# A linear-attention and feed-forward kernel: the last tile's stores issued from ScalarE, the first k and v in 64 partitions, and the casts of k^T v and of w_out's units in other places

## The chip, the core and the metric

The kernel runs on one core of a Trainium2 chip. A core has a matrix engine (TensorE, called PE in the profile; its weight loads are listed apart as PEld), VectorE (DVE), ScalarE (ACT), GpSimd (POOL) and SyncE (SP), which here does nothing but issue transfers. Each engine runs its own instructions in the order of the program, and waits on semaphores for the others. The metric is the device time of one execution in microseconds (us).

## The reference

```python
kv = np.einsum('bhsd,bhse->bhde', k, v)              # b=8, h=8, s=576, d=64
out = np.einsum('bhsd,bhde->bhse', q, kv)
rms = np.sqrt(np.mean(out * out, axis=-1, keepdims=True) + 1e-06)
attn = out / rms * g_norm
x = attn.transpose(0, 2, 1, 3).reshape(4608, 512)
h = x @ w_in                                          # 512 x 2048
sp = np.where(h > 20.0, h, np.log1p(np.exp(np.minimum(h, 20.0))))
g = h * np.tanh(sp)                                   # mish
return (g @ w_out).astype(np.float32)                 # 2048 x 512
```

Linear attention over 8 batches of 8 heads, a norm over each head's 64 channels, and a feed-forward of 4608 tokens with mish between its two products. w_in and w_out are float64, which the kernel reads as pairs of 32-bit words; all else is float32.

## The kernel before

**Tiles.** The 4608 tokens go in 9 tiles of 512 (NT = 9). In the first part of the program each tile goes through x @ w_in and mish, and the result g is stored to DRAM (the tiles gd). The second part, from about 530 us on, loads g again and multiplies it by w_out. A product of two 32-bit matrices is made of three matmuls with each operand split into a high part (ACT, CAST, L117) and a low rest (DVE, subtraction, L118). On top of this each product is a Strassen-Winograd scheme: 7 products of half-size blocks instead of 8, with sums of blocks made before and after.

**Slots.** A tile has 4 groups of 7 products, so NS = 28 slots. The schedule is written by hand: slot(t) first runs what `then(t, ...)` has put down (copies and additions that empty a PSUM bank), then its product (12 matmuls for each of two columns, L471 in `mm_in`), then what `at(t, ...)` has put down. That order is the order of every engine's queue. In a group, `p0` to `p6` leave copies behind: ACT copies the bank a to ula (L434, block 11), the bank bc to ur (L439, block 22) and a to ur (L448, block 12); DVE adds a later bank on top of each (L491), ACT takes the mish (L114). `put_in` then stores the blocks to gd: ula (L494), ur (L497) and ulb (L489). The products that accumulate further in bank a wait for the copy at L448.

**Attention.** That of tile j is computed within tile j-1's slots: loads of q (L280), transposes (L285), q times kv (L308 to L313), squares (L318), the sums over a head by PE (L335 to L346), and at slot 16 the reciprocal root by ACT's Ln and Exp (L357, L358), which need another function table than mish: a table load stands before Ln (L356) and another before the next mish (L114). k^T v of batch b is made two tiles ahead: `kv_load` (L211, L212) loads k and v of two heads in 128 partitions and a rest in 64, `kv_product` (L232) multiplies, `kv_keep` brings the result from PSUM to kv in two halves of partitions, each with a cast (L117, ACT) and a rest (L118, DVE); for the first batches it copies to kvf (L249).

**w_out.** It is prepared in 16 units, spread over tiles 1 to 7, at the slots in `places`. A unit has seven steps: load (L134), scale (L139, ACT), join (L144 to L146, DVE: two words become a float), differences (L154 to L156, DVE), blocks and sums (casts wst<-wx and wst<-w on ACT, rests on DVE), and store (wod<-wst, L198, SP). The pools wx and wst have one buffer, so a unit's first cast waits until the store of the unit before has landed. w_in's units j = 0 to 7 go through the same steps at the start, into buffers wf, which stay in use to the end of tile 8. There are eight wf buffers; after the last use of a pair `wo_load` loads w_out's finished forms into them (wf<-wod, L662). The first block of 256 tokens of the second part (s = 0) is multiplied at L790 within the last tile, the others at L708.

**Queues.** All transfers before are issued by SP, in program order. Each takes one of eight semaphores in turn, and waits for the transfer eight before it to land.

Of the kernel before, what the change touches and what calls it, by code (L numbers as in the profile page):

```python
# [7 lines left out]
F32 = mybir.dt.float32  # L8
# [18 lines left out]
def linear_attention_rms_mish_ffn(  # L27
# [33 lines left out]
    nc = tc.nc  # L61
# [62 lines left out]
    def weight_forms(srcs, m, n, room, forms, put=None):  # L124

        st = {}
        w = m * n

        def load():
            t = room()  # L130
            n_ = 4 // len(srcs)
            for i, src in enumerate(srcs):
                dst = t[:, i].rearrange("p (m n) t -> p m (n t)", m=m) if n_ == 1 else t[:, n_ * i:n_ * i + n_].rearrange("p b n t -> p b (n t)")
                nc.sync.dma_start(dst, src)  # L134
            st["w"] = t.rearrange("p b n t -> p (b n) t")
# [12 lines left out]
        def differences():  # L148
            x = st["x"].rearrange("p (b n) -> p b n", b=4)
            if put:  # L150
                d = st["w"].rearrange("p n t -> p (n t)").bitcast(F32)[:, 0:4 * w].rearrange("p (b n) -> p b n", b=4)
            else:
                d = pools["wd"].tile([P, 4, w], F32, name="wd")
            nc.vector.tensor_sub(d[:, 0:2], x[:, 1:4:2], x[:, 0:2])  # L154
            nc.vector.tensor_sub(d[:, 2], x[:, 3], d[:, 0])
            nc.vector.tensor_sub(d[:, 3], x[:, 2], d[:, 2])  # L156
            st["x"], st["d"] = x, d
# [7 lines left out]
        def blocks():  # L165
            parts(B11, B11 + 1, st["x"][:, 0:1])
            parts(B21, B22 + 1, st["x"][:, 2:4])
# [316 lines left out]
    def put_in(st, block, bank, t):  # L484
        o, i, n = u_dst(st, block), st["i"], st["n"]
        left, right = gd[i][:, 2 * n:2 * n + 2, :], gd[i][:, NF2 + 2 * n:NF2 + 2 * n + 2, :]
        if block == "21":
            mish(o, bank)
            at(t + 2, lambda: nc.sync.dma_start(left[:, :, TH:T], o))  # L489
            return  # L490
        nc.vector.tensor_add(o, bank, o)  # L491
        if block == "11":
            then(t + 1, lambda: mish(o, o))
            at(t + 3, lambda: nc.sync.dma_start(left[:, :, 0:TH], o))  # L494
        elif block == "22":
            then(t + 1, lambda: mish(st["r"], st["r"]))
            at(t + 3, lambda: nc.sync.dma_start(right, st["r"]))  # L497
# [9 lines left out]
    rooms = [up.tile([P, 4, CM * D], F32, name="ur") for _ in range(2)]  # L507
    rooms += [x[:, 2 * u:2 * u + 2].rearrange("p a (h n) -> p (a h) n", h=2) for u in range(2)]
    rrooms = [up.tile([SL, 4, D], F32, name=n) for n in ("ula", "ula", "ulb", "ulb")]

    early = {j: wfp.tile([P, 4, 2 * P, 2], U32, name="wf") for j in range(1, 4)}
    early_q = wfp.tile([P, 2, T // R * D], F32, name="wf")
# [4 lines left out]
    conv = {j: weight_in(j, (lambda j=j: early[j]) if 0 < j < 4 else w64_room) for j in range(NF2)}  # L517
# [41 lines left out]
    kv_product(0, 0, 4, *kv0[0])  # L559
# [320 lines left out]
```

## Time and profile before

| what | us |
|---|---|
| median of 3 runs | 900.79 |
| lowest, highest | 899.94, 905.96 |
| the profiled execution, whole | 899.57 |
| its span on the core | 897.8 |
| PE busy in it | 831.1 |
| DVE busy | 613.7 |
| ACT busy | 459.2 |

A row of a timeline has the start, the time, the engine, the line, the operation and the tiles written and read, with how many instructions went into the row; in brackets stands the idle time of that engine before it, and what ended it. A row of the waits has the engine and line that waited, what released it, and three numbers: us in total, times, and the longest. A granted clock (PEclk) under 1.00 means that PE ran part of that stretch at a lower clock. The chain of work that ended last runs in PE's second part almost without a break.

### The profile page before, as it was taken

What the parts mean: (1) busy time and instruction counts of PE and PEld (TensorE: products, weight loads), DVE (VectorE), ACT (ScalarE), POOL (GpSimd) and SP (SyncE); (2) the same over time, 40 slices, a digit from 0 to 9 for tenths busy, and PEclk for the clock granted to TensorE, in tenths of its full rate; (3) what the DMA queues carried; (4) which work ended last, traced back from release to release, by engine and by line L of the source; (5) the groups of instructions that cost most, each with busy time, mean ns of one, the idle gap of its engine ahead of it and who ended that gap; (6) DMA issues with size and microseconds to landing.
All of it is one profiled execution on the core that took longest, in us unless ns stands there. A gap on an engine that the chain in (4) does not pass through costs nothing. (4 is left out here: it accounts for less than half of the span.)

```text
span 897.8 us, 17035 instructions
## 1 busy us (share of the span) xinstructions
PE 831.1 (93%) x6940; PEld 796.0 (89%) x6940; DVE 613.7 (68%) x808; ACT 459.2 (51%) x698; POOL 4.3 (0%) x21
## 2 busy tenths in 40 slices
PE   1678899998999999999999699999999999999997
PEld 1366699888999999999899699999999999999997
DVE  4688675776767767676765258877676767777672
ACT  2465656566576655666675244443444443443441
POOL 1000000000000000000000000000000000000000
PEclk9988999998999999999999899999999999999999
DMA  9958598978879796867657996333444344333421
GB/s 242 264 149 234 171 279 248 263 231 248 268 235 293 230 268 194 234 206 202 205 173 239 408 376 226 119 118 118 151 153 144 118 135 124 118 118 120 157 77 48
DMA packets 157134, 177.41 MB, mean 198 GB/s; under 512 B 18752, under 2 KB 138560, under 8 KB 156032
## 3 DMA queue, kind: packets, MB, share of 16 engines
q1 hardware_dynamic: 157056, 176.33, 64.8%
q8 instruction: 54, 0.88, 0.4%
q14 instruction: 24, 0.20, 0.1%
HBM read 114.30 MB, written 62.00 MB: 196 GB/s over the span
## 5 line engine op out<-in xcount | busy, mean ns | idle before, releaser
L708 PE MATMUL a<-wf,gf 128*128 128x256 f32 x1632 | 201.8, 283 | 0.5 <-DVE ur L739 0.5
L708 PEld LDWEIGHTS a<-wf,gf 128*128 128x128 f32 x1632 | 198.4, 192 | 0.7 <-DVE ur L739 0.7
L118 DVE TENSOR_TENSOR gf<-g,gf 128x1024 fp32r<-128x1024 f32 (+1 forms) x123 | 132.8, 1087 | 88.0 <-ACT gf L117 88.0
L471 PE MATMUL a<-gf,wf 128*128 128x256 f32 x1296 | 177.3, 291 | 12.2 <-ACT ur L448 9.4
L471 PEld LDWEIGHTS a<-gf,wf 128*128 128x128 f32 x1296 | 166.5, 197 | 20.0 <-ACT ur L448 11.5
L471 PE MATMUL bc<-gf,wf 128*128 128x256 f32 x1296 | 170.8, 286 | 8.4 <-ACT ur L439 7.4
L471 PEld LDWEIGHTS bc<-gf,wf 128*128 128x128 f32 x1296 | 162.4, 192 | 10.1 <-ACT ur L439 7.6
L117 ACT CAST gf<-g 128x1024 fp32r<-128x1024 f32 (+1 forms) x123 | 114.4, 939 | 90.6 <-DVE g L688 65.1
L708 PE MATMUL bc<-wf,gf 128*128 128x256 f32 x1224 | 152.7, 283 | 0.1
L708 PEld LDWEIGHTS bc<-wf,gf 128*128 128x128 f32 x1224 | 149.4, 192 | 0.3 <-ACT gf L117 0.3
L471 PE MATMUL a<-a,wf 128*128 128x256 f32 x432 | 59.3, 288 | 6.2 <-DVE ur L491 6.2
L471 PEld LDWEIGHTS a<-a,wf 128*128 128x128 f32 x432 | 55.9, 194 | 10.0 <-DVE ur L491 4.9
L114 ACT ACTIVATE ur<-ur 128x1024 f32<-128x1024 f32 x36 | 38.1, 1059 | 40.4 <-DVE ur L491 40.2
L118 DVE TENSOR_TENSOR fa<-fl,fh 128x1024 fp32r<-128x1024 f32 x28 | 34.2, 1222 | 22.1 <-ACT fh L117 21.2
L118 DVE TENSOR_TENSOR gf<-gf 128x512 fp32r<-128x512 f32 x45 | 30.4, 689 | 23.9 <-ACT gf L117 23.9
L439 ACT COPY ur<-bc 128x512 f32<-128x512 f32 (+1 forms) x53 | 27.4, 517 | 36.1 <-PE bc L708 22.7
L117 ACT CAST gf<-a 128x1024 fp32r<-128x1024 f32 x17 | 17.9, 1052 | 53.3 <-DVE a L685 53.3
L448 ACT COPY ur<-a 128x512 f32<-128x512 f32 (+1 forms) x53 | 27.4, 517 | 32.9 <-PE a L708 24.6
L117 ACT CAST gf<-gf 128x512 fp32r<-128x512 f32 x45 | 27.1, 619 | 32.3 <-DVE gf L395 19.1
L491 DVE TENSOR_TENSOR ula<-bc,ula 128x512 f32<-128x512 f32 x36 | 24.7, 687 | 23.5 <-PE bc L471 18.2
L114 ACT ACTIVATE ula<-ula 128x512 f32<-128x512 f32 x36 | 22.8, 632 | 29.7 <-DVE ula L491 29.6
L117 ACT CAST fh<-fl 128x1024 fp32r<-128x1024 f32 x28 | 29.4, 1048 | 0.0
(134 smaller groups left out, 842.0 us busy)
## 6 DMA issues: line engine op xcount, KB each, us to landing
g<-gd SPq DMA_DIRECT2D x18, 2048.0 KB, 8.7
gd<-ur SPq DMA_DIRECT2D x36, 512.0 KB, 4.5
wod<-wst SPq DMA_DIRECT2D x16, 896.0 KB, 6.9
wf<-wod SPq DMA_DIRECT2D x8, 1792.0 KB, 15.0
gd<-ula SPq DMA_DIRECT2D x36, 256.0 KB, 4.6
gd<-ulb SPq DMA_DIRECT2D x36, 256.0 KB, 5.0
w<-in_moe_w_out_dram SPq DMA_DIRECT2D x32, 256.0 KB, 5.2
km<-in_k_dram SPq DMA_DIRECT2D x28, 256.0 KB, 4.6
```

What stands on the lines that cost most here:

```text
L114: nc.scalar.activation(o, i, AF.Mish)
L117: nc.scalar.copy(hi, src)
L118: nc.vector.tensor_sub(lo, src, hi.bitcast(F32))
L439: then(t + 2, lambda: nc.scalar.copy(dst(st, "22"), st["c"]))
L448: then(t + 4, lambda: nc.scalar.copy(dst(st, "12"), st["a"]))
L471: nc.tensor.matmul(bank[:, jj], w[:, right, a, kc, :], xf[:, b, kc, :], start=first and jj == kc == s == 0, stop=(kc == 1 and s == 2), ski ...
L491: nc.vector.tensor_add(o, bank, o)
L708: nc.tensor.matmul(bank, gf[:, a, c, :], wo[c][:, right, b, :], start=first and c == s == 0, stop=(c == NF2 - 1 and s == 2), skip_group_ch ...
```

## The change

There are four parts.

1. The first batch's k and v (b = 0) are loaded by `kv_first` for four heads at a time: 64 partitions, each with 9 tokens in a row (2304 bytes), one transfer each for k and v, into wf buffers that are free at that time. `kv_first_product` multiplies 9 chunks of 64 rows. Before, four heads came as 4 chunks of 128 rows in 1024-byte rows and a rest of 64 rows in 256-byte rows, into buffers of ur, ula, gf and ulb. w_in's units are loaded in 2 transfers of 512 KB instead of 4 of 256 KB, and the sums and blocks of a unit read the blocks in the new order. In ACT's order the sums of w_in's unit 1 and the first square stand ahead of the second copy of kv.
2. `kv_keep` makes both casts first and then both rests; from batch 3 on the loads, the products and the keep stand earlier (the keep at slot 11 instead of 14).
3. w_out's units have their blocks, sums and store a slot earlier; units at slot 15 have join, differences, blocks, sums and store at +1, +2, +4, +4 and +7.
4. The last tile's twelve stores to gd are issued by ACT.

```diff
 def weight_forms(srcs, m, n, room, forms, put=None):
...
-            n_ = 4 // len(srcs)
-            for i, src in enumerate(srcs):
-                dst = t[:, i].rearrange("p (m n) t -> p m (n t)", m=m) if n_ == 1 else t[:, n_ * i:n_ * i + n_].rearrange("p b n t -> p b (n t)")
-                nc.sync.dma_start(dst, src)
+            for src, places in srcs:
+                nc.sync.dma_start(t[:, places].rearrange("p b (m n) t -> p (b m) (n t)", m=m), src)
...
+    def kv_first(h0):
+        ts = []
+        for src in (k, v):
+            t = wfp.tile([S // 9, 4, 9 * D], F32, name="wf")
+            nc.sync.dma_start(t, src[0, h0:h0 + 4].rearrange("h (p c) d -> p h (c d)", c=9))
+            ts.append(t)
+        return ts
+
+    def kv_first_product(h0, kt, vt):
+        for i in range(2):
+            for c in range(9):
+                for o in range(2):
+                    d = slice(c * D, (c + 1) * D)
+                    nc.tensor.matmul(kvps[o * D:(o + 1) * D, 0, h0 // 2 + i, :], kt[:, 2 * i + o, d], vt[:, 2 * i + o, d], start=(c == 0), stop=(c == 8))
...
+        t = kvt[b % 2]
         for r in (slice(0, D), slice(D, P)):
-            if b >= T32 - 1:
-                split(kvt[b % 2][r, 0, n, r], kvt[b % 2][r, 1, n, r], kvps[r, b % 2, n, :])
+            nc.scalar.copy(t[r, 0, n, r], kvps[r, b % 2, n, :])
+        for r in (slice(0, D), slice(D, P)):
+            nc.vector.tensor_sub(t[r, 1, n, r], kvps[r, b % 2, n, :], t[r, 0, n, r].bitcast(F32))
...
+        eng = nc.sync if i < NT - 1 else nc.scalar
...
-            at(t + 3, lambda: nc.sync.dma_start(left[:, :, 0:TH], o))
+            at(t + 3, lambda: eng.dma_start(left[:, :, 0:TH], o))
...
-    weights(1, DIFF, BLOCKS)
-    kv_product(0, 4, 4, *kv0[1])
+    weights(1, DIFF, BLOCKS, SUMS)
+    do(0, 0, "square")
+    kv_first_product(4, *kv0[1])
     kv_keep(0, slice(2, 4))
-    do(0, 0, "square", "sums")
-    weights(1, SUMS)
+    do(0, 0, "sums")
...
-        loads = (5, 6, 14, 16) if b == 2 else (20 - NS, 22 - NS, 5, 8) if b == 3 else (11 - NS, 15 - NS, 5, 8)
+        loads = (5, 6, 14, 16) if b == 2 else (20 - NS, 22 - NS, 4, 6) if b == 3 else (8 - NS, 10 - NS, 4, 6)
...
-            at(t + ((12, 14, 16, 18) if b == 2 else (3, 6, 9, 12))[p], lambda b=b, p=p: k_product(b, p))
-        at(t + (20 if b == 2 else 14), lambda b=b: kv_keep(b, slice(0, NKC)))
+            at(t + ((12, 14, 16, 18) if b == 2 else (2, 4, 6, 8))[p], lambda b=b, p=p: k_product(b, p))
+        at(t + (20 if b == 2 else 11), lambda b=b: kv_keep(b, slice(0, NKC)))
...
-        for s, n in zip(range(7), (-12, 0, 0, 1, 2, 3, 5)):
+    places = [(NS * j + n, (0, 1, 2, 4, 4, 7) if n == 15 else (0, 0, 1, 1, 2, 4)) for j in range(1, NT - 1) for n in ((6, 13, 20) if j < 3 else (9, 15))]
+    for i, (t, ns) in enumerate(places):
+        for s, n in zip(range(7), (-12,) + ns):
```

In the order of the instructions the change shows at three places. The first is ACT at the start: kvf is k^T v of the first batch (s is its PSUM tile), wf takes the forms of w_in's units 0 and 1, fa the square of the first tile's attention. Before:

```order
L249 COPY kvf_181<-s_122 64x2x64 x2
L117 CAST wf<-fl 128x256
L117 CAST wf<-fl 128x2x256
L117 CAST wf<-wd 128x4x256
L139 ACTIVATE fl<-wf 128x1024
L117 CAST wf<-fl 128x256
L117 CAST wf<-fl 128x2x256
L249 COPY kvf_181<-s_122 64x2x64 x2
L318 ACTIVATE fa<-x_247 128x1024
L117 CAST wf<-wd 128x4x256
```

After the change:

```order
L263 COPY kvf_167<-s_122 64x2x64 x2
L117 CAST wf<-fl 128x256
L117 CAST wf<-fl 128x2x256
L117 CAST wf<-wd 128x4x256
L138 ACTIVATE fl<-wf 128x1024
L117 CAST wf<-fl 128x256
L117 CAST wf<-fl 128x2x256
L117 CAST wf<-wd 128x4x256
L336 ACTIVATE fa<-x_249 128x1024
L263 COPY kvf_167<-s_122 64x2x64 x2
```

The second copy of kvf went behind the last cast of unit 1 and the square.

The second place is ACT in tile 1, around Ln and Exp. kv is k^T v of a later batch, wx and w hold a w_out unit, wst its forms; ur, ula and ulb are the blocks of g. Before:

```order
L117 CAST kv_187<-s_122 64x4x64 x2
L114 ACTIVATE ur<-ur 128x1024
L434 COPY ula<-a 128x512
L117 CAST wst<-wx 128x128
L117 CAST wst<-wx 128x2x128
L439 COPY ur<-bc 128x2x256
L356 ACT_TABLE_LOAD
L357 ACTIVATE fl<-ss,eps 8x512
L358 ACTIVATE fl<-fl 8x512
L117 CAST wst<-w_1157 128x4x128
L114 ACT_TABLE_LOAD
L114 ACTIVATE ulb<-a 128x512
```

After the change:

```order
L138 ACTIVATE wx<-w_1167 128x512
L117 CAST wst<-wx 128x128
L117 CAST wst<-wx 128x2x128
L114 ACTIVATE ur<-ur 128x1024
L452 COPY ula<-a 128x512
L117 CAST wst<-w_1167 128x4x128
L457 COPY ur<-bc 128x2x256
L374 ACT_TABLE_LOAD
L375 ACTIVATE fl<-ss,eps 8x512
L376 ACTIVATE fl<-fl 8x512
L114 ACT_TABLE_LOAD
L114 ACTIVATE ulb<-a 128x512
```

The kv casts went ahead of the piece, to where the group before ends; the casts wst<-wx went from behind the copy of ula to ahead of the mish, and the cast wst<-w from between Exp and the table load to ahead of the copy ur<-bc.

The third place is SP at the start of the last tile, whose g is gd_102. Before:

```order
L667 DMA g<-gd_94 128x16x256 x2
L494 DMA gd_102<-ula 128x2x256
L662 DMA wf<-wod_103 128x3584
L662 DMA wf<-wod_104 128x3584
L497 DMA gd_102<-ur 128x1024
L489 DMA gd_102<-ulb 128x2x256
L494 DMA gd_102<-ula 128x2x256
L662 DMA wf<-wod_105 128x3584
L662 DMA wf<-wod_106 128x3584
L497 DMA gd_102<-ur 128x1024
```

After the change:

```order
L679 DMA g<-gd_94 128x16x256 x2
L674 DMA wf<-wod_103 128x3584
L674 DMA wf<-wod_104 128x3584
L674 DMA wf<-wod_105 128x3584
L674 DMA wf<-wod_106 128x3584
L674 DMA wf<-wod_107 128x3584
L674 DMA wf<-wod_108 128x3584
L674 DMA wf<-wod_109 128x3584
L674 DMA wf<-wod_110 128x3584
```

and the stores stand in ACT's queue among the copies that fill and empty the same buffers (PSUM banks a and bc):

```order
L452 COPY ula<-a 128x512
L513 DMA gd_102<-ula 128x2x256
L457 COPY ur<-bc 128x2x256
L114 ACTIVATE ulb<-a 128x512
L516 DMA gd_102<-ur 128x1024
L466 COPY ur<-a 128x2x256
L508 DMA gd_102<-ulb 128x2x256
```

Twelve stores left SP, where they had stood between the loads of g and of wf, for ACT.

More of the change, by code (lines that the diff above doesn't have):

```diff
@@ L153, in differences @@
                 d = pools["wd"].tile([P, 4, w], F32, name="wd")
-            nc.vector.tensor_sub(d[:, 0:2], x[:, 1:4:2], x[:, 0:2])
+            nc.vector.tensor_sub(d[:, 0:2], x[:, 2:4], x[:, 0:4:2])
             nc.vector.tensor_sub(d[:, 2], x[:, 3], d[:, 0])
-            nc.vector.tensor_sub(d[:, 3], x[:, 2], d[:, 2])
+            nc.vector.tensor_sub(d[:, 3], x[:, 1], d[:, 2])
             st["x"], st["d"] = x, d
@@ L166, in blocks @@
             parts(B11, B11 + 1, st["x"][:, 0:1])
-            parts(B21, B22 + 1, st["x"][:, 2:4])
+            parts(B21, B22 + 1, st["x"][:, 1:4:2])
         def sums():
@@ L183, in weight_in @@
         srcs = []
-        for kh, r in ((0, 0), (0, 1), (1, 0), (1, 1)):
+        for r in range(2):
             c0 = 2 * P * (j + r * NF2)
-            src = w_in[kh * 2 * P:(kh + 1) * 2 * P, c0:c0 + 2 * P]
-            srcs.append(src.rearrange("(m p) n -> p m n", p=P))
+            srcs.append((w_in[:, c0:c0 + 2 * P].rearrange("(m p) n -> p m n", p=P), slice(2 * r, 2 * r + 2)))
         return weight_forms(srcs, 2, P, room, forms)
@@ L201, in weight_out @@
             f0 = (c + fh * NF2) * P
-            srcs.append(w_out[f0:f0 + P, :].rearrange("p (r h n) -> p r h n", r=2, h=2)[:, :, h, :])
+            srcs.append((w_out[f0:f0 + P, :].rearrange("p (r h n) -> p r h n", r=2, h=2)[:, :, h, :], slice(fh, 4, 2)))
         return weight_forms(srcs, 1, P, room, forms, store)
@@ L249, in kv_keep @@
                 nc.scalar.copy(kvf[b][r, n, r], kvps[r, b % 2, n, :])
+        if b < T32 - 1:
+            return
+        t = kvt[b % 2]
         for r in (slice(0, D), slice(D, P)):
-            if b >= T32 - 1:
-                split(kvt[b % 2][r, 0, n, r], kvt[b % 2][r, 1, n, r], kvps[r, b % 2, n, :])
+            nc.scalar.copy(t[r, 0, n, r], kvps[r, b % 2, n, :])
+        for r in (slice(0, D), slice(D, P)):
+            nc.vector.tensor_sub(t[r, 1, n, r], kvps[r, b % 2, n, :], t[r, 0, n, r].bitcast(F32))
     def segments(j):
@@ L488, in put_in @@
             mish(o, bank)
-            at(t + 2, lambda: nc.sync.dma_start(left[:, :, TH:T], o))
+            at(t + 2, lambda: eng.dma_start(left[:, :, TH:T], o))
             return
@@ L506, in linear_attention_rms_mish_ffn, with wf_room @@
     open_pools(wst, ("w64", 1), ("wd", 1), ("kvf", 1))
[L507 to L512, printed above, removed]
     def w64_room():
         return pools["w64"].tile([P, 4, 2 * P, 2], U32, name="w64")
-    conv = {j: weight_in(j, (lambda j=j: early[j]) if 0 < j < 4 else w64_room) for j in range(NF2)}
+    def wf_room():
+        return wfp.tile([P, 4, 2 * P, 2], U32, name="wf")
+    conv = {j: weight_in(j, wf_room if 0 < j < 4 else w64_room) for j in range(NF2)}
     LOAD, SCALE, JOIN, DIFF, BLOCKS, SUMS, STORE = range(7)
@@ L532, in linear_attention_rms_mish_ffn @@
     nc.scalar.preload_act_table_set("natural_log_exp_and_others")
-    kv0 = []
-    def k_first(n):
-        kv0.append(kv_load(nc.sync, 0, 4 * n, 4, [t for m in range(2) for t in (rooms[2 * n + m], rrooms[2 * n + m])]))
     weights(0, LOAD)
-    k_first(0)
+    kv0 = [kv_first(0)]
     weights(1, LOAD)
     do(0, 0, "load")
-    k_first(1)
-    units[0][1]["load"](early_q)
+    kv0.append(kv_first(4))
+    units[0][1]["load"](wfp.tile([P, 2, T // R * D], F32, name="wf"))
     for r in (slice(0, D), slice(D, P)):
@@ L558, in linear_attention_rms_mish_ffn @@
     weights(0, SCALE, JOIN)
-    kv_product(0, 0, 4, *kv0[0])
+    kv_first_product(0, *kv0[0])
     kv_keep(0, slice(0, 2))
@@ L635, in linear_attention_rms_mish_ffn @@
     at(NS - 2, out_pools)
-    places = [NS * j + n for j in range(1, NT - 1) for n in ((6, 13, 20) if j < 3 else (9, 15))]
-    for i, t in enumerate(places):
-        for s, n in zip(range(7), (-12, 0, 0, 1, 2, 3, 5)):
+    places = [(NS * j + n, (0, 1, 2, 4, 4, 7) if n == 15 else (0, 0, 1, 1, 2, 4)) for j in range(1, NT - 1) for n in ((6, 13, 20) if j < 3 else (9, 15))]
+    for i, (t, ns) in enumerate(places):
+        for s, n in zip(range(7), (-12,) + ns):
             def run(i=i, s=s):
```

2 lines of the change are left out of this document (1 added, 1 removed).

## Prediction

> **What bounds the kernel now.** I read the busy times first, then a table of stretches of the span, then what TensorE (PE) waits for, then the timeline around each long wait.
>
> ```profile
> span 897.8 us, 17035 instructions
> PE 831.1 (93%) x6940; PEld 796.0 (89%) x6940; DVE 613.7 (68%) x808; ACT 459.2 (51%) x698; POOL 4.3 (0%) x21
> ```
>
> The change takes no matmul of the big products away, so all that can be won is PE's 67 us of idle time and its half-speed stretches. Where they lie, by stretch (start:end, length, busy us of each engine with its instruction count, granted PE clock, DMA share, GB/s):
>
> ```profile
> core 0: us, PE busy (x) PEld busy (x) DVE busy (x) ACT busy (x) POOL busy (x), PEclk, DMA share, GB/s
> 0.00:50.00 50.00, 19.31 (x160) 11.70 (x160) 30.02 (x41) 21.84 (x33) 4.32 (x21) 1.00 0.99 249
> 50.00:118.00 68.00, 57.97 (x447) 47.84 (x448) 55.10 (x74) 38.52 (x58) 0.00 (x0) 0.87 0.67 189
> 118.00:186.00 68.00, 65.15 (x580) 61.96 (x578) 48.41 (x76) 42.20 (x69) 0.00 (x0) 0.97 0.90 269
> 186.00:254.00 68.00, 64.00 (x562) 60.65 (x559) 47.19 (x77) 41.13 (x67) 0.00 (x0) 0.95 0.84 246
> 254.00:322.00 68.00, 67.17 (x601) 63.88 (x600) 48.06 (x75) 43.92 (x70) 0.00 (x0) 1.00 0.81 242
> ...
> 390.00:458.00 68.00, 65.79 (x512) 62.25 (x512) 49.66 (x74) 44.10 (x70) 0.00 (x0) 1.00 0.61 184
> 458.00:526.00 68.00, 58.57 (x468) 57.75 (x467) 28.42 (x49) 32.04 (x55) 0.00 (x0) 0.95 0.85 303
> ...
> 600.00:898.00 298.00, 292.47 (x2436) 292.07 (x2434) 202.48 (x200) 118.34 (x155) 0.00 (x0) 1.00 0.39 119
> ```
>
> The reader should see five different places: a start that is bound by DMA (share 0.99), a stretch short of work and clock up to 118, two stretches (tiles 1 and 2) with about 3 and 4 us idle and a lower clock, tiles 3 to 7 nearly full, and 9.4 us idle in the last tile. The long tail is full and the change leaves it alone. What PE waited for (us in total, times, longest):
>
> ```profile
> PE s L232 <- DMA ur<-in_v_dram: 11.9, 1, 11.9
> PE a L471 <- ACT ur L448: 9.4, 8, 3.6
> ...
> PE bc L471 <- ACT ur L439: 7.4, 1, 7.4
> ...
> PE s L232 <- DMA vm<-in_v_dram: 4.9, 1, 4.9
> ```
>
> Each of the four parts of the change aims at one of these lines.
>
> **Part 1: first k and v in 64 partitions.** It moves the same 1.18 MB for each of the two groups of four heads, as 2 transfers into 64 partitions instead of 4 into 128 and 64. Transfers into few partitions show in the trace: 15 to 18 us is the load of q into 32 partitions, 30 to 33 that of w_in into 128, 7 to 12 holds k and v as they are now.
>
> ```profile
> 7.00:12.00 5.00, 0.07 (x2) 0.10 (x4) 3.08 (x3) 1.12 (x1) 0.00 (x0) 1.00 1.10 291
> 15.00:18.00 3.00, 0.00 (x0) 0.00 (x0) 1.63 (x3) 2.94 (x6) 0.00 (x0) 1.00 1.03 228
> 30.00:33.00 3.00, 1.95 (x4) 0.68 (x4) 2.10 (x2) 2.45 (x4) 0.00 (x0) 1.00 1.00 320
> ```
>
> 1.18 MB takes 4.1 us at 291 GB/s, 5.2 at 228 and 3.7 at 320: from -0.4 to +1.1 a group. I take +1.1, because q's rows have long packets and few partitions, as the new loads have. [...]
>
> The product of four heads goes from 40 records (4 chunks of 128 rows and a rest, for each pair) to 72 of 64 rows:
>
> ```profile
> 11.93 1.12 PE L232 MATMUL s<-ur 128*64 128x64 f32 x16 [11.93 <-DMA ur<-in_v_dram]
> 12.98 0.48 PE L232 MATMUL s<-ula 64*64 64x64 f32 x4
> ```
>
> At 1.12/16 = 0.07 us each 72 cost 5.0 us, without the change of shape, which is the excess of the second row (0.48 for 4, against 0.28), 4.2; before it was 1.12+0.48 twice, about 3.0. So +1.2 to +2.0 for the first group. The first unit's sums and the squares stand ahead of the second copy of kv afterwards, and no longer wait for its product; that covers the second product's longer run and most of the first's delay. What is left is the load time: two groups late by 1.1 each push the wait on vm (4.9 us) by 2.2, and about half of that is absorbed, because the chain behind it up to 71 us is held by VectorE (DVE), not by PE. I take **+1.0**, with ends -0.8 (both groups at 320 GB/s) and +4.6 (1.1 of load and 1.2 of product for each group, nothing absorbed).
>
> **Part 2 in the stretch 50 to 118, and w_in in half as many transfers.** ScalarE (ACT) no longer waits between the two halves of the kv cast. The other waits there are loads and DVE, which stay, so of the 3.2 us of that wait (row 149.66 below) only a quarter is counted: **-0.8** (-2 to +1).
>
> **Parts 2 and 3 in tiles 1 and 2.** ACT's timeline in tile 1, up to the copy PE waits for (start, us, in brackets the idle time before and its releaser), the matmuls around that copy, those around it in tile 2, a long and a short wait in the last tile, the issue of tile 1's store of w_out's forms and the landing of all such stores:
>
> ```profile
> 149.66 0.37 ACT L117 CAST kv<-s 64x256 fp32r<-64x256 f32 x1 [3.23 <-DVE kv L118]
> ...
> 151.14 0.59 ACT L434 COPY ula<-a 128x512 f32<-128x512 f32 x1
> 152.56 0.61 ACT L117 CAST wst<-wx 128x128 fp32r<-128x128 f32 x2 [0.84 <-DMA wod<-wst]
> ...
> 156.22 0.60 ACT L117 CAST wst<-w 128x512 fp32r<-128x512 f32 x1
> ...
> 158.62 0.58 ACT L448 COPY ur<-a 128x512 f32<-128x512 f32 x1
> ```
> ```profile
> 159.26 4.62 PE L471 MATMUL a<-gf,wf 128*128 128x256 f32 x24 [2.48 <-ACT ur L448]
> ...
> 208.46 3.04 PE L471 MATMUL bc<-gf,wf 128*128 128x256 f32 x24
> 215.06 5.49 PE L471 MATMUL a<-gf,wf 128*128 128x256 f32 x24 [3.56 <-ACT ur L448]
> ...
> 510.48 2.93 PE L471 MATMUL bc<-gf,wf 128*128 128x256 f32 x12 [7.44 <-ACT ur L439]
> ...
> 517.64 1.69 PE L471 MATMUL bc<-gf,wf 128*128 128x256 f32 x12 [0.95 <-DVE ula L491]
> ```
> ```profile
> 147.10 0.60 SPq L198 DMA_DIRECT2D wod<-wst  x1
> ```
> ```profile
> DMA to landing us min/median/max: 4.9/6.9/8.9
> ```
>
> The whole stake: 2.48 + 3.56 = 6.0 us idle, and 24 matmuls at 4.62 and 5.49 instead of 3.04, 1.6 + 2.4 = 4.0 more; together 10.0. The clock falls behind the long waits and not behind the wait of 0.95.
>
> The kv casts go to a place where ACT is idle, which frees 3.2 us. But the casts wst<-wx now stand ahead of the mish, of the copy ula<-a and of the copy ur<-bc, and they still wait for the store of the unit before, since wst has one buffer. Casts and store are each a slot earlier. The store took 5.5 us (issued 147.1, by the bracket of row 152.56 landed by 152.56); issued near 146 it lands at 150.9 at the least. From there: two casts 0.61, mish 1.06, copy 0.59, cast wst<-w 0.60, copy ur<-bc 0.58, then tables, Ln and Exp without the cast, 3.9, and ulb 0.5: the copy ur<-a starts near 158.4 instead of 158.62. So one wait takes the place of the other. In tile 2 the same sum gives 0.6. Idle: -0.9 in all. But PE now loses the time in two pieces, at ur<-bc and at ur<-a, of about 1 and 1.5 us, and shorter waits did not lower the clock; I count two thirds of the 4.0: -2.6. Together **-3.5**, ends -10.0 (the store lands before the casts want it) and +1.5 (it lands at 8.9 behind the moved loads of k and v).
>
> **Parts 2 and 3 in tiles 3 to 7.** From 254 to 458 PE waited thus:
>
> ```profile
> PE a L471 <- ACT ur L448: 2.4, 5, 0.6
> ```
>
> By the stretches above the idle time there is 0.8 in one and 2.2 in another. These waits stand behind the kv casts (3.2) and the cast beside Exp (0.6), which both go; the later offsets at slot 15 leave ACT free there. **-2.5** (-3.5 to +1).
>
> **Part 4: the last tile.** A store on SP stood behind two loads of g, 2 MB each, and two loads wf<-wod; ACT waited for its landing, and PE for ACT:
>
> ```profile
> 486.77 5.84 SPq L494 DMA_DIRECT2D gd<-ula  x1
> ...
> 493.93 0.44 SPq L497 DMA_DIRECT2D gd<-ur  x1
> ```
> ```profile
> 509.84 0.58 ACT L439 COPY ur<-bc 128x512 f32<-128x512 f32 x1 [9.98 <-DMA gd<-ur]
> ```
> ```profile
> 484.00:545.00 61.00, 51.71 (x411) 50.90 (x410) 24.86 (x57) 24.29 (x50) 0.00 (x0) 0.94 1.01 379
> 503.00:510.50 7.50, 0.06 (x2) 0.02 (x1) 0.00 (x0) 0.66 (x2) 0.00 (x0) 0.79 1.04 415
> ```
> ```profile
> g<-gd SPq DMA_DIRECT2D x18, 2048.0 KB, 8.7
> ...
> wf<-wod SPq DMA_DIRECT2D x8, 1792.0 KB, 15.0
> ```
>
> Issued from ACT the stores pass SP's backlog. At stake are 7.44 us and the half clock behind it, 2.93 instead of 1.6, 8.8 together. But DMA is full for those 61 us, and the last products of the first block need the last wf<-wod. 61 us at 379 GB/s are 23.1 MB; at 415, the best stretch, 55.7 us: the last load can come at most 5.3 us earlier, and at 395 2.5. PE wins its 8.8 before and gives most back ahead of the last products. [...] ACT takes over 12 issues of about 0.4 us in return; they lie in its idle time (51% busy). I take **-2.5**, ends -5.3 and, with ACT held by its own stores as SP was for 5.84, +3.
>
> **Sum.** +1.0 - 0.8 - 3.5 - 2.5 - 2.5 = -8.3. The profiled execution took 899.57 (span 897.8 and 1.8 around it), 1.2 under the median of the runs, 900.79: 891.3, so **891 us**.
>
> **Rivals.** (a) *The stalls go whole.* The store lands before the casts want it, and the loads move at 415 GB/s: -10.0 and -5.3 instead of -3.5 and -2.5, 899.57 + 1.0 - 0.8 - 10.0 - 2.5 - 5.3 = 882. For it: ACT has 3.2 us more in each tile. Against it: the bracket of row 152.56, and the DMA share.
>
> (b) *The change doesn't do what it says.* The wait for the store keeps tiles 1 and 2 as they were, clock included, and the last tile gives all back: 899.57 + 1.0 - 0.8 - 2.5 = 897. For it: the replay, which won only 0.2 and 0.6 of idle time.
>
> (c) *Slower: ACT is held by its own stores.* In the program's order each transfer has one of eight semaphores, in turn, and waits at the head of its engine's queue for the transfer eight before it; SP stood 5.84 us in this way at a store. Where ACT's stores share a semaphore with wf<-wod (15.0 us to land), ACT stands, with the copies behind it. Of a hold of 9.98 PE lost 7.44, so a hold of 15.0 costs 12.5, and 1.3 of clock. Two of them: 27.6 against 8.8 before, +19, with -5.8 from the other terms 913. It decides for slower by over 1% from two holds of 13.6 us on (24.8 of loss, +16).
>
> (d) *The 64-partition loads cost their upper end*, +4.6 and the stretch behind it +1, with (b) elsewhere: 899.57 + 4.6 + 1.0 - 2.5 = 903. Against it: ACT's new order, which takes the second product off the path.
>
> **Chances.** Forecast 0.47 (its own terms, 886 to 896); (a) 0.20; (b) 0.21; (c) 0.06; (d) 0.06. The range reaches into (a) and over (b): 882.5 to 899. One per cent, 9 us, is about what a measurement of this kernel can tell from no change: faster is below 891.8, half of the forecast's case and all of (a), 0.45; slower is (c) and a bit of (d), 0.08; the same 0.47.
>
> **What would show it.** Start: the first k^T v later than 11.93 by 1.1; sooner, and the loads were fast. Tiles 1 and 2: two waits of 1 to 1.5 us each in place of 2.48 and 3.56, the 24 matmuls behind at about 3.0; a wait of the casts wst<-wx on wod. Last tile: no wait of 7.4 us near 503, one of some us ahead of the last products of the first block, on wf<-wod. The prediction is wrong if ACT stands at an issue in the last tile, or if the casts find their buffer free.

## The result and the profile after

The changed kernel takes 893.22 us (median of 7 runs, 892.54 to 894.53), and 0.990 of the time before (95% interval 0.988 to 0.992). The ratio is taken from undisturbed runs alone, so it does not follow from the median of all seven runs of before beside it, 904.73. The prediction was 891. The profiled execution took 892.98 (span 891.2), 6.6 us less than that of before, where the prediction's sum said 8.3.

The page of the changed kernel, its busy times:

```profile
span 891.2 us, 17127 instructions
PE 829.7 (93%) x7004; PEld 796.6 (89%) x7004; DVE 614.2 (69%) x808; ACT 460.8 (52%) x698; POOL 4.3 (0%) x21
```

PE's busy time is nearly the same (831.1 before, with 64 small matmuls fewer); its idle time fell from 67 to 61.5 us. What PE waited for in the changed kernel (us in total, times, longest):

```profile
PE s L228 <- DMA wf<-in_v_dram: 13.2, 1, 13.2
...
PE s L246 <- DMA vm<-in_v_dram: 6.6, 3, 5.5
PE a L489 <- ACT ur L466: 4.7, 4, 2.0
...
PE bc L489 <- ACT ur L457: 2.4, 1, 2.4
PE a L489 <- ACT ula L452: 2.2, 2, 1.4
...
PE bc L720 <- DVE gf L118: 1.3, 2, 0.8
```

Read beside the list of before: the copy of a (now L466) went from 9.4 to 4.7, the copy of bc (L457) from 7.4 to 2.4. The first load went up from 11.9 to 13.2 and that of vm from 4.9 to 6.6. Two lines are new: the copy to ula, and the low rests that DVE makes (L118) in the second part.

How much that is, stage by stage, shows best by counting. The first part has 3024 matmuls of x and w_in in both traces, the second 2856 at its main line, so the n-th of one can be set against the n-th of the other. The table has the start of a matmul (us) and how long each stretch took, changed minus before:

| up to | before | changed | stretch | predicted |
|---|---|---|---|---|
| first matmul of x and w_in | 40.64 | 41.66 | +1.02 | +1.0 |
| tile 1 | 120.91 | 120.96 | -0.97 | -0.8 |
| tile 3 | 232.00 | 229.36 | -2.69 | -3.5 |
| tile 8 | 476.55 | 472.49 | -1.41 | -2.5 |
| first matmul of s = 1 | 549.00 | 540.76 | -4.18 | -2.5 |
| its 169th | 569.51 | 562.69 | +1.42 | |
| the last | 892.71 | 885.90 | +0.01 | 0 |

### The profile page after: what moved, and what is told of

Read it like the earlier page. It is cut to its first block, busy times and chain, and to the rows that moved or that the text cites. A ratio compares the mean times of both kernels' runs of the same rounds, so it can differ in the third digit from the quotient of the medians.

```text
span 891.2 us, 17127 instructions
## 1 busy us (share of the span) xinstructions
PE 829.7 (93%) x7004; PEld 796.6 (89%) x7004; DVE 614.2 (69%) x808; ACT 460.8 (52%) x698; POOL 4.3 (0%) x21
## 4 chain that ended last, share of the span: by engine, by line
PE 65%; DMA 10%; DVE 10%; ACT 8%; issue 4%; SPq 1%; ACTq 0%; DVEq 0%
PE a L720 21%; PE bc L720 16%; PE a L489 14%; PE bc L489 8%; DMA gd<-ula 4%; PE s L246 2%; DVE ur L510 1%; DMA wf<-in_v_dram 1%; DMA gd<-ur 1%; DMA w<-in_moe_w_in_dram 1%; DMA vm<-in_v_dram 1%; DVE gf L118 1%; ACT L374 1%; ACT gf L117 1%; ACT L114 1%
## 5 line engine op out<-in xcount | busy, mean ns | idle before, releaser
L118 DVE TENSOR_TENSOR gf<-g,gf 128x1024 fp32r<-128x1024 f32 (+1 forms) x123 | 133.0, 1087 | 89.4 <-ACT gf L117 89.4
L489 PE MATMUL a<-gf,wf 128*128 128x256 f32 x1296 | 175.3, 289 | 10.1 <-ACT ur L466 4.7
L118 DVE TENSOR_TENSOR fa<-fl,fh 128x1024 fp32r<-128x1024 f32 x28 | 34.2, 1223 | 19.6 <-ACT fh L117 18.6
L118 DVE TENSOR_TENSOR gf<-gf 128x512 fp32r<-128x512 f32 x45 | 30.3, 689 | 23.0 <-ACT gf L117 23.0
L457 ACT COPY ur<-bc 128x512 f32<-128x512 f32 (+1 forms) x53 | 27.4, 517 | 31.7 <-PE bc L720 23.0
L466 ACT COPY ur<-a 128x512 f32<-128x512 f32 (+1 forms) x53 | 27.4, 516 | 30.3 <-PE a L720 24.6
L510 DVE TENSOR_TENSOR ur<-bc,ur 128x512 f32<-128x512 f32 x36 | 24.4, 678 | 11.3 <-PE bc L489 5.7
```

The source lines that it names most:

```text
L118: nc.vector.tensor_sub(lo, src, hi.bitcast(F32))
L457: then(t + 2, lambda: nc.scalar.copy(dst(st, "22"), st["c"]))
L466: then(t + 4, lambda: nc.scalar.copy(dst(st, "12"), st["a"]))
L489: nc.tensor.matmul(bank[:, jj], w[:, right, a, kc, :], xf[:, b, kc, :], start=first and jj == kc == s == 0, stop=(kc == 1 and s == 2), ski ...
```

## The experiments

All runs are set against this ledger, since it keeps stages apart that a total adds up. Each column is the length of a stretch minus that of before, in us; the time is a median:

| kernel | start | to tile 1 | tiles 1, 2 | tiles 3 to 7 | last tile | s = 1 | time |
|---|---|---|---|---|---|---|---|
| changed | +1.02 | -0.97 | -2.69 | -1.41 | -4.18 | +1.42 | 893.22 |
| changed, again | +1.27 | -1.01 | -2.55 | -1.91 | -4.01 | +1.40 | 892.83 |
| before with part 4 | +1.37 | +2.02 | -1.25 | +0.02 | -4.07 | +1.13 | 898.17 |
| without part 4 | +4.65 | -1.75 | -2.59 | -1.50 | -0.38 | -0.01 | 895.88 |
| without part 3 | +4.51 | -2.09 | -3.23 | +2.18 | -4.28 | +1.12 | 898.10 |
| without part 2 | +1.66 | -0.30 | -2.71 | -2.23 | -4.08 | +1.13 | 893.80 |
| first k, v in 128 | -0.25 | -0.30 | -2.93 | -1.47 | -4.39 | +1.40 | 889.49 |
| casts behind Exp | +4.27 | -0.82 | -4.76 | -0.69 | -4.21 | +1.12 | 892.07 |
| stores on SP, loads behind | +4.89 | -1.42 | -2.23 | -1.72 | -2.81 | -0.35 | 894.30 |
| 128, and casts behind | -2.63 | -2.36 | -5.51 | -0.28 | -4.39 | +1.13 | 886.14 |
| changed, added matmuls | +10.41 | -0.26 | -3.21 | -0.54 | -4.21 | +1.13 | 902.02 |
| 128, casts behind, added | +7.13 | -0.18 | -3.59 | -0.85 | -3.95 | +1.12 | 897.82 |
| the same, in a bank apart | +0.02 | -0.03 | -4.88 | +3.72 | -4.50 | +1.13 | 892.53 |

Stretches whose code is that of before show what chance does: "before with part 4" differs by +1.37, +2.02 and -1.25 in the first three, and by 0.02 in the fourth. The fourth is not safe from chance either: the last row has +3.72 there where the row of the same code without added matmuls has -0.28, nearly all of it in tile 3, behind a wait of 2.36 us for a load of v.

**Part 4 alone, on the kernel before.** The line `eng = nc.sync if i < NT - 1 else nc.scalar` and its three uses, nothing else.

> The kernel before with part 4 alone (the last tile's twelve stores issued by ACT). Theory (the stores' place in SP's queue is what cost the time, and its gain is independent of the rest): the wait of 7.4 us near 503 goes, the first product of the second part's block s = 1 comes 4.2 us earlier than before (549.0 to about 544.8), of which 1.4 us is given back within the next 20 us: 2.8 us in all, about 897. Rival (most of the last tile's gain comes from the tile being reached earlier, so that its loads meet other traffic): under 1 us, 899 to 900.

898.17 us, 0.996 of before (0.994 to 0.998). The wait of 7.4 us fell to 2.3, s = 1 begins 4.07 us earlier relative to tile 8, and 1.13 of it is given back within s = 1: 2.9 net. That is the theory's 2.8, and independent of the other parts.

**Part 4 undone.**

```diff
-        eng = nc.sync if i < NT - 1 else nc.scalar
+        eng = nc.sync
```

> The changed kernel with part 4 undone (all stores on SP). Theory: the 2.8 us come back, about 896, with a wait of 6 to 8 us at the copy of bank bc in the last tile and the time up to the last tile as in the changed kernel. Rival: within 1 us of the changed kernel's 893.

895.88 us, 0.993 (0.990 to 0.996). Its longest wait in the last tile:

```profile
PE bc L489 <- ACT ur L457: 7.2, 1, 7.2
```

The old wait is back, and the last tile takes 0.38 us less than before instead of 4.18: 2.4 net by the ledger. Both sides agree.

**The engine or the place in the queue?** The stores go back to SP, but g's loads and the loads wf<-wod are written behind the stores of their group.

```diff
-        eng = nc.sync if i < NT - 1 else nc.scalar
+        eng = nc.sync
...
-    at(t8 + 7, lambda: g_load(0))
-    at(t8 + 8, lambda: g_load(1))
+    at(t8 + 9, lambda: g_load(0))
+    at(t8 + 13, lambda: g_load(1))
...
-            at(t8 + 7 * n + 10, lambda c=2 * n + m: wo_load(c))
+            at(t8 + 7 * n + 13, lambda c=2 * n + m: wo_load(c))
```

> The changed kernel with the last tile's stores on SP, but the two loads of g and the loads wf<-wod written behind the stores of their group (2 to 5 slots later). Theory (it is the place in the queue that counts, not the engine that issues): the waits of the last tile fall as with ACT's stores, the second part's s = 1 begins within 1 us of 4.2 us earlier relative to tile 8's start, or the later loads give up to 3 us of it back in front of the last products: 893 to 895. Rival (ACT's stores profit from a queue of their own, beside SP's): a wait of 5 us or more at the copy of bank bc stays, 896 or more.

894.30 us, 0.993 (0.990 to 0.995), after a late start. Last tile and s = 1 together: -3.16 us, against -2.76 with ACT's stores. Its longest waits there:

```profile
PE a L489 <- ACT ula L452: 2.9, 1, 2.9
PE q L802 <- DMA wf<-wod: 1.8, 2, 1.5
```

So the gain comes from the place in the queue; ACT is only one way to it. In these runs the engine itself brought nothing (-2.76 us with it, -3.16 without); what it brought is another place in an order that was blocked.

**Part 3 undone.** Offsets of w_out's units as before.

```diff
-    places = [(NS * j + n, (0, 1, 2, 4, 4, 7) if n == 15 else (0, 0, 1, 1, 2, 4)) for ...
+    places = [(NS * j + n, (0, 0, 1, 2, 3, 5)) for ...
```

> The changed kernel with part 3 undone (w_out's units at the old offsets). Theory (the casts of a unit wait for the store of the unit before, so where they stand decides, and moving the kv casts alone frees time that this wait takes again): tiles 1 and 2 have waits of 2.5 and 3.5 us at the copy of a again and their gain of 2.7 us is lost, as is most of the 1.4 us of tiles 3 to 7: about 896.5. Rival (the kv casts were what held the copy): waits of under 1 us in tiles 1 and 2, 891 to 893.

898.10 us, 0.996 (0.994 to 0.998), 4.9 above the changed kernel. The theory's total came out, for another reason. In tiles 1 and 2 the waits are back, as it said:

```profile
160.99 4.58 PE L489 MATMUL a<-gf,wf 128*128 128x256 f32 x24 [2.29 <-ACT ur L466]
...
215.21 4.63 PE L489 MATMUL a<-gf,wf 128*128 128x256 f32 x24 [3.12 <-ACT ur L466]
```

yet the stretch is 3.23 us shorter than before, no worse than in the changed kernel. Of the loss against the changed kernel, 3.6 us lie in tiles 3 to 7, which take 2.18 more than before, and 2.4 in the start, which came late in this profile as it did in some others with the same code. In tiles 3, 4 and 5 PE's wait at the copy of a is 1.13 to 1.17 us each, where before it was 0.41 to 0.42 and in the changed kernel none is listed:

```profile
318.38 3.14 PE L489 MATMUL a<-gf,wf 128*128 128x256 f32 x24 [1.17 <-ACT ur L466]
```

**Part 2 undone.** `kv_keep` with cast and rest in turn, and k and v at their old slots.

```diff
         for r in (slice(0, D), slice(D, P)):
-            nc.scalar.copy(t[r, 0, n, r], kvps[r, b % 2, n, :])
-        for r in (slice(0, D), slice(D, P)):
-            nc.vector.tensor_sub(t[r, 1, n, r], kvps[r, b % 2, n, :], t[r, 0, n, r].bitcast(F32))
+            split(t[r, 0, n, r], t[r, 1, n, r], kvps[r, b % 2, n, :])
```

> The changed kernel with part 2 undone (kv casts and rests in turn, at the old slots). Theory (in tiles 1 and 2 the wait for the store hides the wait of the kv casts: ACT would be free of kv at about 150.0 and of the store at 149.8): tiles 1 and 2 lose under 0.7 us; tiles 3 to 7 lose 1 to 1.5 us, and the stretch up to 118 up to 1 us: 894.5 to 896. Rival (the kv casts alone bring tiles 1 and 2): 3 us there, 897 or more.

893.80 us, 0.991 (0.988 to 0.993): no difference from the changed kernel that can be told. Tiles 1 and 2 keep their gain, as the theory had it, but tiles 3 to 7 do not lose, they gain 0.3 to 0.8 more. So in tiles 3 to 7 part 3 without part 2 does what both were credited with (-2.23), and part 2 without part 3 costs 2.2 us. In tiles 1 and 2 either part may be missing without a loss (-2.71 and -3.23), so what each brings there stays open.

**The wait for the store.** In tiles 1 and 2 the casts of the unit at slot 13 go behind Exp, and the unit at slot 20 follows.

```diff
-(0, 1, 2, 4, 4, 7) if n == 15 else (0, 0, 1, 1, 2, 4)
+(0, 1, 2, 4, 4, 7) if n == 15 else (0, 1, 2, 5, 5, 8) if n == 13 else (0, 1, 2, 5, 5, 7) if n == 20 else (0, 0, 1, 1, 2, 4)
```

> The changed kernel, in tiles 1 and 2 the unit at slot 13 has its casts wst<-wx and wst<-w behind Exp and behind the copy of a (offsets 0, 1, 2, 5, 5, 8), and the unit at slot 20 follows it (0, 1, 2, 5, 5, 7). Theory (in the changed kernel it is the wait for the landing of the unit's store before, 3.00 and 4.47 us, that holds the copies in tiles 1 and 2): no wait of PE on ACT over 0.5 us there, full clock in tile 1, 2.0 + 1.6 + 1.4 + 1.5 = 6.5 us less, less 0.5 to 1 that the later casts cost elsewhere: 887 to 888. Rival (the mish waits for DVE and the copies for Ln, Exp and two table loads anyway): waits of 1.5 us or more stay in each tile, 891 or more.

892.07 us, 0.990 (0.987 to 0.993), against 0.990 for the changed kernel: not told apart. Tiles 1 and 2 take 4.76 us less than before, 2.1 more won than in the changed kernel, and tiles 3 to 7 give 0.7 back. In tile 2 PE no longer waits for ACT. In tile 1 another store steps in:

```profile
155.69 0.59 ACT L457 COPY ur<-bc 128x512 f32<-128x512 f32 x1 [2.68 <-DMA gd<-ur]
```

The theory's 6.5 us were too much: behind one late store stands the next. With the same casts in the last version of this section PE did wait in tile 2, for 2.47 us, behind the same kind of store:

```profile
200.77 0.59 ACT L457 COPY ur<-bc 128x512 f32<-128x512 f32 x1 [3.42 <-DMA gd<-ur]
```

**The first k and v in 128 partitions.** The changed kernel with `kv_load` and `kv_product` for the first batch, in the buffers they had before.

```diff
-    kv0 = [kv_first(0)]
+    k_first(0)
...
-    kv_first_product(0, *kv0[0])
+    kv_product(0, 0, 4, *kv0[0])
```

> The changed kernel with the first k and v loaded and multiplied as before (128 partitions and rests in the buffers of ur, ula, gf and ulb), all else as changed, ACT's new order at the start too. Theory (the form with 64 partitions costs 1.0 to 1.3 us of loading and 1.1 us of product for the first group, and its longer second product keeps PE longer in its cold state): first v there at 11.9 instead of 13.2, the first product of x and w_in at 38.5 to 40 instead of 41.7, and about 1 us of it left at the end: 891.5 to 892.5. Rival (what the start loses is absorbed by the waits up to 118, as 1.0 of the 1.0 was in the changed kernel's profile): tile 1 begins at the same 121 us, 893 within 0.5.

889.49 us, 0.987 (0.982 to 0.991). The same stretch of time, 7 to 12 us, in the changed kernel and in this one (start:end, length, busy us of each engine, clock, DMA share, GB/s):

```profile
7.00:12.00 5.00, 0.00 (x0) 0.00 (x0) 4.44 (x6) 0.35 (x1) 0.00 (x0) 1.00 1.05 204
```
```profile
7.00:12.00 5.00, 1.11 (x18) 1.02 (x18) 4.23 (x5) 0.60 (x1) 0.00 (x0) 1.00 1.11 305
```

Both have a full DMA share; one moves 204 GB/s, the other 305. When PE starts, in the changed kernel and here:

```profile
13.19 4.11 PE L228 MATMUL s<-wf 64*64 64x64 f32 x72 [13.19 <-DMA wf<-in_v_dram]
```
```profile
10.89 1.12 PE L246 MATMUL s<-ur 128*64 128x64 f32 x16 [10.89 <-DMA ur<-in_v_dram]
```

Before, it was 11.93 (11.90 with part 4 alone). The first issues on SP, before and here:

```profile
0.74 1.99 SPq L134 DMA_DIRECT2D w<-in_moe_w_in_dram  x4
```
```profile
0.74 1.01 SPq L133 DMA_DIRECT2D w<-in_moe_w_in_dram  x2
```

So part 1 is two effects. With w_in in half as many transfers, two issues of about 0.5 us fewer stand ahead, and the load of v is issued at 3.13 instead of 4.07; v is there about 1.0 us earlier in this profile. The 64 partitions bring it 2.3 us later. Neither is fixed: the four profiles with this start have v at 10.4, 10.9, 11.0 and, in one, 12.3, and the eight with 64 partitions at 13.1 to 13.7. The 204 against 305 GB/s at a full share go the same way as these 2.3 us, but in a stretch in which other loads run too: what the 64 partitions alone cost in rate was not shown.

**The changed kernel again**, unaltered, beside the next two.

> The changed kernel once more, unaltered, on the same chip as the three others. Theory (the start has two states by chance): first product of x and w_in at 41.7 or at 45, and a median of 893 to 895. Rival (its first profile was typical): 41.5 to 42.5, 893.2 within 0.5.

892.83 us, 0.993 (0.990 to 0.995); first matmul at 41.91. But the same start came out in two ways. The second group's k^T v, in the changed kernel again and in the one without part 4, whose start is the same code:

```profile
29.07 2.43 PE L228 MATMUL s<-wf 64*64 64x64 f32 x72
31.43 1.99 PE L353 MATMUL bc<-fa,ones 128*128 128x512 f32 x4
33.25 1.88 PE L326 MATMUL a<-fh,kvf 128*128 128x512 f32 x4
```
```profile
29.47 4.11 PE L228 MATMUL s<-wf 64*64 64x64 f32 x72
33.51 3.78 PE L353 MATMUL bc<-fa,ones 128*128 128x512 f32 x4
37.08 2.42 PE L326 MATMUL a<-fh,kvf 128*128 128x512 f32 x4
```

PE runs these rows one behind the other, and up to the third they take 4.18 us in one and 7.61 in the other. That is the 3.4 us by which the one first matmul of x and w_in comes later.

Of the seven profiles with this start, three have the first matmul of x and w_in at 41.7 to 42.3 and four at 44.9 to 45.5. The four with 128 partitions and no added matmuls have it at 38.0 to 42.0.

**Is it PE's cold state?** The same rows can take up to twice as long at the start: the four matmuls at L353 took 3.78 us without part 4 and 1.99 in the changed kernel, with the granted clock at 1.00 from 30 to 40 us in both. That is called cold here, and warm where they are short. Added matmuls (ones times zeros; their result is not used) in PE's idle time behind the first k^T v.

```diff
     kv_first_product(0, *kv0[0])
+    for i in range(16):
+        nc.tensor.matmul(kvps[:, 1, :, :], ones, kvf[1][:, 0:2, :], start=True, stop=True)
```

> The changed kernel with 16 more matmuls (128x256, ones times zeros, into the half of the PSUM tile that batch 1 overwrites) behind the first group's k^T v, in the 8 us in which PE waits for the first transposed q. Theory (what spreads the start by 3 to 4 us between executions of the same program is PE's state: in the profiles where the second group's product took 4.11 us the first product of x and w_in came at 45, in that where it took 2.57 at 41.7): with PE kept busy the four matmuls at 25.5 take about 1.9 instead of 3.75, the product 2.6 at most, the first product of x and w_in starts at 40 or sooner, and the median falls by 1 to 3 us against the changed kernel on the same chip. Rival (the chain of DVE, ACT and DMA sets the start anyway, or the added matmuls delay it): the first product at 41.5 or later, the median within 0.7 us of the changed kernel or above it.

902.02 us, 1.002 (1.000 to 1.004). The experiment failed: the added matmuls write the PSUM tile that ACT's copy of kvf reads, the copy waited for them, and the start came 9.4 us later.

```profile
17.47 9.37 PE L572 MATMUL s<-kvf,ones 128*128 128x256 f32 x32
35.03 3.75 PE L326 MATMUL x<-fh,kvf 128*128 128x512 f32 x4 [8.20 <-DVE fh L303]
```

It shows one thing all the same: the start is 9.4 us later than in the changed kernel, and the last matmul 10.1. Nothing behind absorbed it here. With the version of 128 partitions it went the same way:

> The version with 128 partitions and later casts, with the 16 added matmuls too. Theory: at or under its own form without them, 886 to 888, and with a smaller spread. Rival: the added matmuls bring nothing where the products have 128 rows: within 0.5 us of it.

897.82 us, 0.998 (0.996 to 0.999), with the first matmul at 47.8. Then the same with a PSUM bank of its own:

```diff
+    warm = ps_m.tile([P, 2, TH], F32, name="bc")
+    for i in range(13):
+        nc.tensor.matmul(warm[:, 0], ones, kvf[1][:, 0:2, :], start=True, stop=True)
```

> The version with 128 partitions and later casts, with 13 added matmuls (128x256, ones times zeros) in the same idle stretch of PE, but into a PSUM bank that no other engine reads then: in the two runs with added matmuls the copy of kvf waited for them (28 us instead of 18), since they wrote the tile that it reads, and everything came 9 us later. Theory (PE's cold state costs the start: 32 records took 9.37 us, which is 8 cold ones of 0.47 and 24 warm ones of 0.235): the added matmuls end by 21.5 us, the four matmuls of the first x take about 1.9 instead of 3.75, the second group's k^T v 2.0 instead of 3.1, the first product of x and w_in starts 1.5 to 3 us sooner than in the same version without them, and the median is 1 to 2.5 us lower: 884 to 885. Rival (ACT, DVE and the loads of q set the start): the first product of x and w_in within 0.7 us of it, 886 within 0.7.

892.53 us, 0.989 (0.987 to 0.991), above the 0.987 (0.983 to 0.990) of the version without them, though the intervals overlap. PE was warm for the next product, and the start did not come sooner:

```profile
22.18 1.96 PE L326 MATMUL x<-fh,kvf 128*128 128x512 f32 x4 [0.35 <-DVE fh L303]
```
```profile
30.30 1.25 DVE L303 STREAM_TRANSPOSE fh<-wf 128x1024 f32<-128x1024 f32 x1 [4.43 <-DMA wf<-in_q_dram]
```
```profile
31.69 3.65 PE L326 MATMUL a<-fh,kvf 128*128 128x512 f32 x4 [2.81 <-DVE fh L303]
```

The four matmuls took 1.96 instead of 3.75, and the first matmul of x and w_in came at 40.66, not before 38.01: the second load of q was late, at 30.30 against 28.53. PE waited 2.81 us for it and was cold again: the next four took 3.65, against 1.96 in the version without added matmuls. So the gain of this theory did not come; why the loads differ by 1.8 us between the two was not settled. Nor does the median speak about the start alone, since 4.0 us of this profile's loss against that version lie in tiles 3 to 7, where it waited for a load of v. In the form with 64 partitions the rows above show the price, 3.4 us between a cold and a warm second group; that added matmuls would save it was not shown.

**The version that beats both**: 128 partitions for the first k and v, casts behind Exp in tiles 1 and 2.

> The changed kernel with both edits of the last two experiments: the first k and v in 128 partitions again, and the casts of w_out's units at slots 13 and 20 of tiles 1 and 2 behind Exp. Theory (the two act in different stretches and add up): 3 to 4 us under the changed kernel on the same chip by the start and 1.5 to 2 by tiles 1 and 2: 887 to 889. Rival (the start's gain is that of a lucky execution): 890 to 892.

886.14 us (885.47 to 892.48), 0.987 of before (0.983 to 0.990), where the changed kernel on the same chip had 0.993 (0.990 to 0.995): 6.7 us by the medians. PE starts at 10.37 us.

## Why the prediction came out

**The start: size right by luck, sum wrong.** +1.0 was forecast and +1.02 measured, but by terms that missed each other, and in a profile with one of the better starts. "I take +1.1" for a group's load was half of what it cost: 2.3 us. It was taken over from q's 228 GB/s, but q's four transfers go to four different groups of 32 partitions, and the new loads' stretch ran at 204. What made up for it, the two issues fewer of w_in, was counted nowhere in this term (-1.0). The first product was sized nearly right: 4.11 us instead of 3.0, about +1.1 for "+1.2 to +2.0". The second was costed at nothing, with the reordered ACT as its cover; in four of seven profiles that cover was short by over 3 us, since its 72 records and the four sums behind them were cold (4.11 and 3.78 us without part 4, 2.43 and 1.99 in the changed kernel again). And "about half of that is absorbed" did not hold for later starts: the added matmuls' delay came through whole, and of the starts that were 3.3 to 3.9 us later than the changed kernel's, tile 1 was still 2.4 to 3.4 later. Rival (d), +4.6 at the start, was nearer than its 0.06: those four profiles have +4.3 to +4.9, though only in part by the loads. Without part 1's new form the time falls from 893 to 889.5, with intervals that overlap, and together with the later casts by 6.7 us.

**To tile 1.** -0.8 forecast, -0.97 measured. Other profiles with the same code in this stretch have -0.8 to -2.1, and without part 2 it is -0.3. But it is -0.3 as well in the kernel with the first k and v in 128 partitions, which has part 2, and +2.02 in that with part 4 alone, which has the code of before. So the term is not told from chance.

**Tiles 1 and 2: mechanism seen, credit open.** "So one wait takes the place of the other": ACT now waits for the landing of the unit's store, longer than before, ahead of the mish. ACT in both tiles, then PE in both, then PE in tile 1 of the same kernel's second profile:

```profile
149.83 0.61 ACT L117 CAST wst<-wx 128x128 fp32r<-128x128 f32 x2 [3.00 <-DMA wod<-wst]
...
157.87 0.58 ACT L466 COPY ur<-a 128x512 f32<-128x512 f32 x1
```
```profile
205.45 0.61 ACT L117 CAST wst<-wx 128x128 fp32r<-128x128 f32 x2 [4.47 <-DMA wod<-wst]
```
```profile
158.51 4.63 PE L489 MATMUL a<-gf,wf 128*128 128x256 f32 x24 [2.01 <-ACT ur L466]
```
```profile
207.54 1.70 PE L489 MATMUL a<-gf,wf 128*128 128x256 f32 x12 [1.37 <-ACT ula L452]
209.07 3.04 PE L489 MATMUL bc<-gf,wf 128*128 128x256 f32 x24
213.59 3.14 PE L489 MATMUL a<-gf,wf 128*128 128x256 f32 x24 [1.48 <-ACT ur L466]
```
```profile
159.09 3.14 PE L489 MATMUL a<-gf,wf 128*128 128x256 f32 x24 [1.57 <-ACT ur L466]
```

In tile 2 the loss came in two pieces, 1.37 and 1.48 where 1 and 1.5 were forecast, the first at the copy of ula and not at that of bc, and the clock stayed up (3.14 for 24 matmuls instead of 5.49). In tile 1 it was one wait of 2.01, and the clock fell behind it in one execution and not in the other. Tile 1 took 53.64 and 53.65 us in the two all the same, since small waits came up elsewhere in the second. In tile 2, too, waits of 0.78 for vm and of 0.89 for DVE took back some of what the clock gave. So -3.5 was 0.8 too much. And of the 2.69 measured, 1.25 may be chance, since part 4 alone has -1.25 with the code of before; and either part could be undone without a loss. The 1.48 recurs to the hundredth in several kernels: from the copy of ula on, ACT has a cast, the copy of bc, two table loads, Ln, Exp, a mish and the copy of a (to 213.54 in tile 2), PE only 36 matmuls (to 212.11). Rival (a), in which these waits go whole, came in no run: the most that tiles 1 and 2 won is 5.51, with the casts behind Exp, against its 10.0.

**Tiles 3 to 7: the term was too large.** -2.5 forecast, -1.4 and -1.9 measured. The step that put the waits behind the kv casts (3.2) and the cast beside Exp (0.6) gave both parts the credit. Part 3 without part 2 brings 2.2; part 2 without part 3 costs 2.2, with longer waits at the copy of a. These are single profiles, but the wait is seen in each of tiles 3 to 5.

**Last tile: the gain right, its limit wrong.** PE was to win 8.8 us and to give "most back ahead of the last products", on wf<-wod. It won 9.5 by the last quarter of tile 8 (504.06 against 517.64, of which 4.06 was there before), and did not wait for wf<-wod at all. It gave 5.3 back up to s = 1, in 3.2 us of waits for copies that stood behind late stores on ACT and in the lower clock behind the longer one:

```profile
512.88 0.59 ACT L457 COPY ur<-bc 128x512 f32<-128x512 f32 x1 [4.91 <-DMA gd<-ur]
```
```profile
484.00:545.00 61.00, 55.91 (x446) 55.00 (x446) 29.08 (x59) 24.96 (x51) 0.00 (x0) 0.97 1.01 396
490.00:520.00 30.00, 24.91 (x189) 24.11 (x189) 10.58 (x22) 10.88 (x21) 0.00 (x0) 0.94 1.03 422
```

Over the 61 us for which the estimate allowed 395 GB/s, DMA ran at 396 (379 before), and in the 30 us around the stores at 422. So the rate was forecast well; what was wrong is that the last load would hold PE. Another 1.42 was given back in s = 1, where PE reaches forms that DVE has not finished. Net -2.76 against -2.5: the bound by bytes gave about the right number for the wrong wait. ACT was not held by its own stores (each was issued in 0.34 to 0.39 us), so rival (c) did not happen. The 5.84 us that SP stood at a store before were no wait of that kind either: the transfer eight before it, issued at 466.04, had landed at 474.95. It was SP that took 36 us over the eight loads, now with no store behind any of them:

```profile
484.98 35.99 SPq L674 DMA_DIRECT2D wf<-wod  x8
```

**The sum.** The five terms of -8.3 came to -6.8 up to the last matmul (-6.6 in span): 0.8 was too much in tiles 1 and 2 and 1.1 in tiles 3 to 7, and 0.4 too little in the rest. Both profiles of the changed kernel have one of its better starts, which the forecast could not know. That the total came within 2 us of 891 is so in part luck.

## What to carry to other kernels

Where several waits overlap on one engine, removing one is worth only what the next leaves (in tiles 1 and 2 the later casts brought 2.1 us of an expected 6.5): undo each part alone before crediting it, stage by stage, with counted instructions rather than totals. In these runs the stores that passed a backlog gained by their place in the order, whichever engine issued them (-2.76 us from ACT, -3.16 from SP). A layout that needs fewer transfers can still lose at the start: in 64 partitions instead of 128 the first v was there 2.3 us later, and a late start reached the end with most of its loss (9.4 us at the start were 10.1 at the last matmul).

## What the runs showed of the hardware

- In a stretch with loads into 64 partitions DMA moved 204 GB/s at a full share, with the loads into 128 in the same place 305; the four loads of k and v in 64 took 8.4 to 13.6 us to land.
- w_in in transfers of 512 KB instead of 256 KB, rows of the same length, saved two issues of about 0.5 us ahead of the first v, which was issued at 3.1 instead of 4.1; its product began at 10.4, 10.9, 11.0 and 12.3 in four profiles, against 11.9 in two.
- In tiles 1 and 2 PE's clock fell behind idle times of 2.01, 2.06 and 2.29 us and all from 2.48 to 3.56, and not behind ones of 2.25, 2.27 and 2.47. Where it fell, the next 24 matmuls took 4.29 to 5.49 us, and 12 took 1.89 behind the 2.06; where it did not, 24 took 3.13 (behind the 2.47) and 12 took 1.69 and 1.70. Behind the longest, from 215.1 to 219 us of before, the granted clock was 0.50. About the same idle time falls on either side, and what decides was not shown.
- 32 records of added matmuls took 9.37 us where a warm one takes about 0.235 and a cold one 0.47 (half of the 128x512 ones). By estimate from these three numbers that is some 8 cold ones, 3.7 us, until PE was warm. In the changed kernel's profile the granted clock reads 1.00 up to 50 us, though four 128x512 matmuls take 3.75 us at 25.50 and 1.88 at 33.50.
